# Attention pipelined one chunk deeper, with 64x64 TensorE tiles, whole-array bonus and logits, and two PSUM pairs held for the whole program

## The chip, the cores and the metric

One Trainium2 chip; the program runs on 1 of its cores. The time is the device time of one execution in microseconds (us), lower is better; where several runs are given, their median counts. Engines are named as in the profile: PE is TensorE's matmuls, PEld its weight loads, DVE is VectorE, ACT ScalarE, POOL GpSimd, SP SyncE, which issues most DMAs.

## The reference, cut to what matters

A linear attention with a decaying state feeds a mixture of experts with one expert per token. All is float32.

```python
def _attn_ref(r, k, v, w, u):            # B, H, S, D = 4, 8, 768, 48
    state = zeros((B, H, D, D))
    for t in range(S):
        cur = einsum('bhd,bhe->bhde', u[None] * kt, vt)
        y[:, :, t] = einsum('bhd,bhde->bhe', rt, state + cur)
        state = w[None, :, :, None] * state + einsum('bhd,bhe->bhde', kt, vt)

def _moe_ref(x, w_gate, w_output_gate, w1, w2):   # N, D, E, F = 3072, 384, 8, 1024
    logits = x @ w_gate
    e_idx = argmax(logits, axis=1)
    gate_w = softmax(logits) at e_idx
    eom = 1 / (1 + exp(-(x @ w_output_gate)))
    for e in range(E):
        h = maximum(x[mask] @ w1[e], 0)
        out[mask] = gate_w[mask] * eom[mask, e] * (h @ w2[e])
```

x is y with the heads of a token put side by side. The logits need full float32, since they choose the expert.

## The kernel before, in words

The 3072 tokens are 24 chunks (`NT`) of 128; a sequence of 768 is 6 chunks (`NCH`). A chunk is cut into two halves of 64 tokens (c = 0, 1), and its 8 heads into 4 pairs (q) of two (j = 0, 1). Powers of the decay w are multiplied into r and k beforehand (`prep`, L229, on GpSimd in the loop), so that a half is three plain products:

- `trans` (L254): 8 TensorE transposes of a chunk's scaled r and k, copied from PSUM by ScalarE as RT and KT; `product` (L268): their product rk on VectorE.
- `scores` (L280): KT against RT for each half, 16 calls of 48 rows by 64 columns, into the two-bank PSUM tile `pa`; `causal` (L293) masks them on VectorE into A.
- `state` (L304): k against v for each half, into the other columns of the same `pa`; `carry` (L319) adds the state so far (VectorE) and decays it (GpSimd), once for each half, as T.
- `inter` (L335): RT against T, 16 calls, into the two-bank tile `y`; `intra` (L348): A against v, added to it.
- `coefs` (L359): rk against a small matrix of u, the bonus coefficient of each head; ScalarE copies it with the logits in `strips` (L1328), and `bonus` (L368) is eight ScalarE activations that scale v by it, into vc.
- `output` (L378): VectorE adds y and vc to x, which SP writes to the scratch tensor x_d; then SP loads k, r and v of a chunk five ahead (`load`, `AHEAD`).

State, intra, coefs and logits address the PE array in strips of 32 output columns (`Q32`): state and intra as 64x32 tiles, two calls for what 64 columns hold, coefs and logits as four 128x32 strips. Each float32 matmul call appears in the trace as two weight loads and two matmuls, a transpose as one of each.

The router follows one chunk behind: three transposes of x (`logits_t`, L421), the logits (`logits_into`, L430), and programs of small steps (`Router.group`) for groups of 4 to 6 chunks; `micro` hands their VectorE steps out by a budget, seven times per turn of the loop, and `tensor_slot` their TensorE steps, twice. From turn 18 on two pieces of the first expert's weights are split per turn (`weights0`: ScalarE rounds, GpSimd subtracts the rest). The order of every engine's instructions in this part is the order in which the code is written (`manual_schedule`).

The expert stage: for each of 8 experts x is gathered and transposed, layer 1 runs in eight steps f of nine matmuls (`l1_mm`, L864) and `l1_out` (L877: hh on ScalarE, then hl on VectorE), layer 2 by `l2_rows` or `l2`. Step f writes one half of a two-bank tile: `bank` (L827) takes a new tile for an even f and the other half of it for an odd one, by turns from the two PSUM places that `pa` and `y` had in the attention. Semaphores are generated from the reads and writes of each tile.

Of the kernel before, what the change touches and what calls it, by code (L numbers as in the profile page):

```python
# [8 lines left out]
F32 = mybir.dt.float32  # L9
# [10 lines left out]
C = 128  # L20
NCH = S // C
# [22 lines left out]
Q32 = 32  # L44
# [174 lines left out]
class Attention:  # L219
    def __init__(self, tc, ctx, ps, k, load, x_d):  # L220
# [3 lines left out]
        self.st, self.T, self.vc, self.A, self.rk, self.pa = {}, {}, {}, {}, {}, {}  # L224
# [13 lines left out]
    def first(self):  # L238
# [3 lines left out]
        for n in (1, 0):  # L242
# [3 lines left out]
            RK[n] = self.pw.tile([C, NP, C], F32, name=("RT", "KT")[n])  # L246
# [7 lines left out]
    def trans(self, i):  # L254
# [4 lines left out]
        for n in (0, 1):  # L259
            p = self.ps.tile([C, NP, C], F32, name="ps_t", tag="tr", bufs=2)  # L260
            for q in range(NP):
                nc.tensor.transpose(p[:, q, :], self.st[i][n][:, 2 * q : 2 * q + 2, :], k.ident)
            t = self.pw.tile([C, NP, C], F32, name=("RT", "KT")[n])
            nc.scalar.copy(t, p)  # L264
            out.append(t)
# [9 lines left out]
    def both(self, i):  # L275
        if i not in self.pa:
            self.pa[i] = self.ps.tile([C, 2, 512], F32, name="ps_a", tag="pa", bufs=1)
        return self.pa[i]

    def scores(self, i):  # L280
# [4 lines left out]
        pa = self.both(i)  # L285
# [7 lines left out]
    def causal(self, i):  # L293
        if i >= NT:
# [4 lines left out]
            self.pa[i][:, :, : NP * HB].rearrange("p j (q t) -> p j q t", q=NP),  # L299
# [4 lines left out]
    def state(self, i):  # L304
# [4 lines left out]
        pa = self.both(i)  # L309
        a = NP * HB  # L310
        for q in range(NP):
            for n in range(2):
                for j in range(2):
                    for c in range(1 if i % NCH == NCH - 1 else 2):
                        rows = slice(HB * c, HB * (c + 1))
                        o = pa[HB * j + Q32 * n : HB * j + Q32 * (n + 1), c, a + D * q : a + D * (q + 1)]
                        nc.tensor.matmul(o, Kn[rows, 2 * q + j, Q32 * n : Q32 * (n + 1)], vt[rows, 2 * q + j, :], start=True, stop=True, skip_group_check=True)

    def carry(self, i, c):  # L319
# [4 lines left out]
        U = self.pa[i][:, c, a : a + NP * D].rearrange("p (q e) -> p q e", q=NP)  # L324
# [10 lines left out]
    def inter(self, i):  # L335
        nc = self.tc.nc
        RT = self.st[i][3]
        self.y = self.ps.tile([C, 2, 512], F32, name="ps_y", tag="y", bufs=1)
# [9 lines left out]
    def intra(self, i):  # L348
        nc = self.tc.nc
        vt, A = self.st[i][2], self.A.pop(i)  # L350
        for q in range(NP):
            for j in range(2):
                for n in range(2):
                    for c in range(2):
                        rows = slice(HB * c, HB * (c + 1))
                        o = self.y[HB * c + Q32 * n : HB * c + Q32 * (n + 1), j, D * q : D * (q + 1)]
# [1115 lines left out]
```

## Time and profile before

| | us |
|---|---|
| median of 3 runs | 521.1 |
| lowest and highest run | 520.45 and 526.82 |
| the profiled execution | 525.61 |
| its span, first to last instruction | 523.8 |

| engine | busy us | share of the span | instructions |
|---|---|---|---|
| PE | 402.9 | 77% | 7473 |
| PEld | 367.5 | 70% | 7473 |
| DVE | 224.4 | 43% | 552 |
| ACT | 192.8 | 37% | 505 |
| POOL | 149.7 | 29% | 213 |

The attention loop takes the first 215 us, the expert stage the rest. The two have different limits, so the shares of the whole span say little about either. The profile's times are of the one profiled execution; what lies outside its span is 1.8 us. A line such as L346 is a line of the kernel; a row names the engine, the operation and the tiles, out<-in.

### The profile page before, as it was taken

The numbers are of one execution on the slowest core, as the hardware profiler recorded it, in microseconds if no ns is written. First come the engines' busy times: TensorE is split into PE (matmuls) and PEld (weight loads), VectorE is DVE, ScalarE is ACT, GpSimd is POOL, SyncE is SP. The second block draws the span as 40 slices with busy tenths as digits, with TensorE's granted clock in tenths as the row PEclk, the third lists the DMA queues.
The fourth block names the chain that finished last, engine by engine and source line by source line (L and its number), as shares of the span: only waits on it lengthen the run. The fifth ranks groups of instructions, "written<-read, shape, count | busy, mean of one in ns | idle before, by whom it ended". The sixth has DMA issues, their size and how long they took to land. (4 is left out here: it accounts for less than half of the span.)

```text
span 523.8 us, 17408 instructions
## 1 busy us (share of the span) xinstructions
PE 402.9 (77%) x7473; PEld 367.5 (70%) x7473; DVE 224.4 (43%) x552; ACT 192.8 (37%) x505; POOL 149.7 (29%) x213
## 2 busy tenths in 40 slices
PE   5867776766777687896968888888879788898780
PEld 3756765655666576796967777788869678787680
DVE  4442374375364552364742343433444435334400
ACT  2425353452553634522332432432442424233300
POOL 5533334243342544523130311211212403101010
PEclk9998788988897876799999989989999999898996
DMA  8834445353557423024252342433532623433000
GB/s 144 144 91 102 101 87 110 80 124 81 108 115 194 110 69 104 18 85 151 76 171 61 116 128 93 132 115 99 170 106 81 206 92 115 161 100 121 1 35 18
DMA packets 104991, 55.19 MB, mean 105 GB/s; under 512 B 78911, under 2 KB 102515, under 8 KB 104896
## 3 DMA queue, kind: packets, MB, share of 16 engines
q1 hardware_dynamic: 101472, 44.08, 33.0%
q0 software_dynamic: 3424, 9.82, 5.5%
q8 instruction: 62, 1.02, 0.8%
q14 instruction: 33, 0.27, 0.2%
HBM read 44.45 MB, written 9.76 MB: 103 GB/s over the span
## 5 line engine op out<-in xcount | busy, mean ns | idle before, releaser
L872 PE MATMUL ps_h<-xh,w1h 128*128 128x384 f32 (+4 forms) x216 | 78.6, 364 | 42.6 <-DVE hl L882 41.3
L909 POOL DMA_INDIRECT out_dram<-yo,si x28 | 31.3, 1117 | 180.1 <-ACT yo L906 110.8
L872 PEld LDWEIGHTS ps_h<-xh,w1h 128*128 128x128 f32 x216 | 43.5, 201 | 52.3 <-DVE hl L882 50.5
L873 PE MATMUL ps_h<-xl,w1h 128*128 128x384 f32 (+4 forms) x216 | 75.0, 347 | 0.0
L874 PE MATMUL ps_h<-xh,w1l 128*128 128x384 f32 (+4 forms) x216 | 74.6, 345 | 0.0
L881 ACT ACTIVATE hh<-ps_h 128x384 fp32r<-128x384 f32 (+4 forms) x72 | 34.2, 475 | 105.8 <-PE ps_h L874 97.5
L882 DVE SCALAR_TENSOR_TENSOR hl<-ps_h,hh 128x384 fp32r<-128x384 f32 (+4 forms) x72 | 38.6, 536 | 80.1 <-ACT hh L881 73.7
L815 DVE TENSOR_TENSOR w1l<-raw,w1h 128x768 fp32r<-128x768 f32 x28 | 26.1, 956 | 63.3 <-ACT w1h L814 63.3
L332 POOL TENSOR_TENSOR T<-T,sq 128x192 f32<-128x192 f32 x40 | 20.7, 517 | 111.9 <-DVE T L331 98.7
L272 DVE TENSOR_TENSOR rk<-ps_t,RT 128x512 f32<-128x512 f32 x23 | 15.9, 692 | 67.4 <-ACT KT L264 67.4
L843 POOL DMA_INDIRECT xg<-x_d,gi x28 | 30.0, 1072 | 51.5 <-PE ps_xt L855 36.5
L874 PEld LDWEIGHTS ps_h<-xh,w1l 128*128 128x128 f32 x216 | 43.9, 203 | 0.1
L934 PE MATMUL ps_o<-w2h,hh 128*128 128x384 f32 x128 | 43.6, 341 | 0.0
L873 PEld LDWEIGHTS ps_h<-xl,w1h 128*128 128x128 f32 x216 | 43.4, 201 | 0.1
L936 PE MATMUL ps_o<-w2h,hl 128*128 128x384 f32 x128 | 42.8, 335 | 0.0
L935 PE MATMUL ps_o<-w2l,hh 128*128 128x384 f32 x128 | 42.8, 334 | 0.0
L375 ACT ACTIVATE vc<-v_t,lg 128x48 f32<-128x48 f32 x136 | 32.5, 321 | 0.6
L291 PE MATMUL ps_a<-RT,KT 48*64 48x64 f32 x768 | 20.4, 254 | 13.2 <-ACT KT L264 13.1
L1335 ACT COPY lg<-ps_lg 128x24 f32<-128x24 f32 x18 | 3.2, 178 | 72.3 <-PE ps_lg L434 72.3
L291 PEld LDWEIGHTS ps_a<-RT,KT 48*64 48x64 f32 x768 | 17.1, 163 | 15.9 <-ACT KT L264 15.2
L815 DVE TENSOR_TENSOR w2l<-raw,w2h 128x768 fp32r<-128x768 f32 x28 | 26.8, 956 | 3.2 <-ACT w2h L814 1.9
L357 PE MATMUL ps_y<-v_t,A 64*32 64x48 f32 x1344 | 23.3, 224 | 5.1 <-issue 5.1
(234 smaller groups left out, 823.4 us busy)
## 6 DMA issues: line engine op xcount, KB each, us to landing
raw<-in_moe_w_dram SPq DMA_DIRECT2D x64, 384.0 KB, 3.5
x_d<-x SPq DMA_DIRECT2D x24, 192.0 KB, 2.1
v_t<-in_v_dram SPq DMA_DIRECT2D x21, 192.0 KB, 4.7
k_t<-in_k_dram SPq DMA_DIRECT2D x20, 192.0 KB
r_t<-in_r_dram SPq DMA_DIRECT2D x20, 192.0 KB, 3.4
raw<-in_v_dram SPq DMA_DIRECT2D x3, 192.0 KB
raw<-in_k_dram SPq DMA_DIRECT2D x3, 192.0 KB, 4.4
xg<-x_d,gi POOLq DMA_INDIRECT x28
```

Source lines behind the costliest of these rows:

```text
L291: nc.tensor.matmul(pa[half, j, HB * q : HB * (q + 1)], KT[rows, q, half], RT[rows, q, half], start=True, stop=True, skip_group_check=True)
L375: nc.scalar.activation(vc[:, h, :], vt[:, h, :], AF.Copy, scale=cs[:, h : h + 1])
L815: (eng or nc.vector).tensor_sub(lo, self.raw[i][:, cs], hi)
L872: nc.tensor.matmul(o, wh[:, j, fs], xh, start=(j == 0), stop=False)
L873: nc.tensor.matmul(o, wh[:, j, fs], xl, start=False, stop=False)
L874: nc.tensor.matmul(o, wl[:, j, fs], xh, start=False, stop=(j == KC - 1))
L881: nc.scalar.activation(hh, o, AF.Relu)
L882: nc.vector.scalar_tensor_tensor(hl, o, 0.0, hh, op0=ALU.max, op1=ALU.subtract)
L909: nc.gpsimd.indirect_dma_start(out=self.out, out_offset=bass.IndirectOffsetOnAxis(ap=self.rt.si[:n, q, s : s + 1] if s else self.rt.si0[:n ...
L934: nc.tensor.matmul(o, hh, wh, start=(f == 0), stop=False)
L935: nc.tensor.matmul(o, hh, wl, start=False, stop=False)
L936: nc.tensor.matmul(o, hl, wh, start=False, stop=(f == FC - 1))
```

## The change

In the loop, turn i now transposes chunk i+2 instead of i+1 and forms its state; scores, causal and inter of i+1 stand at the end of the turn, intra and output of i after the coefs and logits instead of before them. Ahead of the loop chunk 1's state, transposes, product and carries and chunk 0's inter are done. `state` and `intra` use 64x64 tiles, `coefs` and `logits_into` the whole array, one call where there were four. `pa` and `y` are allocated once (`k.two`) for the attention and for the layers of the experts; `bank(f)` hands out their four halves in turn. RT has three buffers instead of two, x two instead of three. The rest of the diff passes `self.pa` and `k.two` in place of the tiles taken per chunk.

```diff
         self.tc, self.k, self.ps = tc, k, ps
         self.load, self.x_d = load, x_d
         self.pw = ctx.enter_context(tc.tile_pool(name="att_w", bufs=2))
-        self.st, self.T, self.vc, self.A, self.rk, self.pa = {}, {}, {}, {}, {}, {}
+        self.st, self.T, self.vc, self.A, self.rk = {}, {}, {}, {}, {}
+        self.pa, self.y = k.two
         self.Rn, self.Kn = ([self.pw.tile([C, H, HB], F32, name=f"{nm}{i}", bufs=1) for i in range(n)] for nm, n in (("Rn", 3), ("Kn", 3)))
         for t in self.Kn + self.Rn:
             tc.nc.gpsimd.memset(t[:, :, D:], 0.0)
...
         self.tc.nc.vector.tensor_mul(rk, self.st[i][5], self.st[i][3])
         self.rk[i] = rk
-    def both(self, i):
-        if i not in self.pa:
-            self.pa[i] = self.ps.tile([C, 2, 512], F32, name="ps_a", tag="pa", bufs=1)
-        return self.pa[i]
-
     def scores(self, i):
         if i >= NT:
             return
         nc = self.tc.nc
         RT, KT = self.st[i][3:5]
-        pa = self.both(i)
+        pa = self.pa
         for q in range(NP):
             for j in range(2):
                 rows = slice(HB * j, HB * j + D)
...
             return
         nc = self.tc.nc
         Kn, vt = self.st[i][1:3]
-        pa = self.both(i)
+        pa = self.pa
         a = NP * HB
         for q in range(NP):
-            for n in range(2):
-                for j in range(2):
-                    for c in range(1 if i % NCH == NCH - 1 else 2):
-                        rows = slice(HB * c, HB * (c + 1))
-                        o = pa[HB * j + Q32 * n : HB * j + Q32 * (n + 1), c, a + D * q : a + D * (q + 1)]
-                        nc.tensor.matmul(o, Kn[rows, 2 * q + j, Q32 * n : Q32 * (n + 1)], vt[rows, 2 * q + j, :], start=True, stop=True, skip_group_check=True)
+            for j in range(2):
+                for c in range(1 if i % NCH == NCH - 1 else 2):
+                    rows = slice(HB * c, HB * (c + 1))
+                    o = pa[HB * j : HB * (j + 1), c, a + D * q : a + D * (q + 1)]
+                    nc.tensor.matmul(o, Kn[rows, 2 * q + j, :], vt[rows, 2 * q + j, :], start=True, stop=True, skip_group_check=True)
     def carry(self, i, c):
         if i >= NT or (c == 1 and i % NCH == NCH - 1):
             return
         nc, k = self.tc.nc, self.k
         a = NP * HB
-        U = self.pa[i][:, c, a : a + NP * D].rearrange("p (q e) -> p q e", q=NP)
+        U = self.pa[:, c, a : a + NP * D].rearrange("p (q e) -> p q e", q=NP)
         decay = k.w64.unsqueeze(2).to_broadcast((C, NP, D))
         T = self.pw.tile([C, NP, D], F32, name="T", bufs=5)
         if i % NCH == 0 and c == 0:
...
         self.T[i, c] = T
     def inter(self, i):
+        if i >= NT:
+            return
         nc = self.tc.nc
         RT = self.st[i][3]
-        self.y = self.ps.tile([C, 2, 512], F32, name="ps_y", tag="y", bufs=1)
         T = [None if i % NCH == 0 else self.T[i - 1, 1], self.T[i, 0]]
         for q in range(NP):
             for j in range(2):
...
         vt, A = self.st[i][2], self.A.pop(i)
         for q in range(NP):
             for j in range(2):
-                for n in range(2):
-                    for c in range(2):
-                        rows = slice(HB * c, HB * (c + 1))
-                        o = self.y[HB * c + Q32 * n : HB * c + Q32 * (n + 1), j, D * q : D * (q + 1)]
-                        nc.tensor.matmul(o, A[rows, j, q, Q32 * n : Q32 * (n + 1)], vt[rows, 2 * q + j, :], start=(i % NCH == 0 and c == 0 and q == 0), stop=(q == NP - 1), skip_group_check=True)
+                for c in range(2):
+                    rows = slice(HB * c, HB * (c + 1))
+                    o = self.y[rows, j, D * q : D * (q + 1)]
+                    nc.tensor.matmul(o, A[rows, j, q, :], vt[rows, 2 * q + j, :], start=(i % NCH == 0 and c == 0 and q == 0), stop=(q == NP - 1), skip_group_check=True)
     def coefs(self, i, lg):
         if i >= NT:
             return
         rk = self.rk.pop(i)
         for q in range(NP):
-            for n in range(C // Q32):
-                strip = slice(Q32 * n, Q32 * (n + 1))
-                self.tc.nc.tensor.matmul(lg[strip, 2 * E + 2 * q : 2 * E + 2 * (q + 1)], rk[:, q, strip], self.k.uw[:, q, :], start=True, stop=True, skip_group_check=True)
+            self.tc.nc.tensor.matmul(lg[:, 2 * E + 2 * q : 2 * E + 2 * (q + 1)], rk[:, q, :], self.k.uw[:, q, :], start=True, stop=True, skip_group_check=True)
     def bonus(self, i, cs):
         if i >= NT:
...
     def logits_into(self, pl, xT):
         for j in range(KC):
-            for n in range(C // Q32):
-                strip = slice(Q32 * n, Q32 * (n + 1))
-                self.tc.nc.tensor.matmul(pl[strip, : 2 * E], xT[:, j, strip], self.wg32[:, j, :], start=(j == 0), stop=(j == KC - 1), skip_group_check=True)
+            self.tc.nc.tensor.matmul(pl[:, : 2 * E], xT[:, j, :], self.wg32[:, j, :], start=(j == 0), stop=(j == KC - 1), skip_group_check=True)
     def logits_mm(self, ps, xT, tag):
         pl = ps.tile([C, 512], F32, name="ps_l", tag=tag, bufs=1)
...
         self.ps = ps
         self.op = ctx.enter_context(self.tc.tile_pool(name="m_o", bufs=2))
-    def bank(self, ps, f, name):
-        n, half = f // 2 % 2, f % 2
-        if half == 0:
-            self.two[n] = ps.tile([C, 2, 512], F32, name=f"{name}{n}", tag=("pa", "y")[n], bufs=1)
-        return self.two[n][:, half, :]
+    def bank(self, f):
+        return self.k.two[f // 2 % 2][:, f % 2, :]
     def rows(self, s, q):
         return min(QP, self.caps[s] - q * QP)
...
     ex = Experts(tc, ctx, k, None, w1, w2, x_d, out)
     pctx = ctx.enter_context(ExitStack())
     ps = pctx.enter_context(tc.tile_pool(name="ps", bufs=1, space=PSUM))
+    k.two = [ps.tile([C, 2, 512], F32, name=n) for n in ('ps_a', 'ps_y')]
     with ExitStack() as actx:
         spare = [t[:, a : a + DM] for t in ex.raw for a in (0, DM)] + [ex.xg[0]]
         G = GROUPS[-1][1]
...
         att.prep(2, 0, nc.gpsimd)
         att.prep(2, 1, nc.vector)
         cs0 = [rw.tile([C, 3 * E], F32, name=f"cs{n}") for n in range(2)]
+        att.state(1)
+        att.inter(0)
+        att.trans(1)
+        att.product(1)
+        att.carry(1, 0)
+        att.carry(1, 1)
         strips(-1, None, cs0[0])
         x = None
         for i in range(NT):
             tail = i == NT - 1
-            att.trans(i + 1)
             xT = None
             if x is not None:
                 xT = rt.logits_t(ps, rw, x, "lg", 1)
             micro(i)
-            att.product(i + 1)
+            att.trans(i + 2)
+            att.prep(i + 3, 0, nc.gpsimd)
+            att.prep(i + 3, 1, nc.gpsimd)
             if tail:
                 ex.early_x(ps)
+            att.product(i + 2)
             tensor_slot(1)
-            att.inter(i)
-            att.scores(i + 1)
             micro(i)
             micro(i)
-            att.causal(i + 1)
-            att.prep(i + 3, 1, nc.gpsimd)
-            att.prep(i + 3, 0, nc.gpsimd)
-            att.intra(i)
-            micro(i)
-            x = att.output(i)
-            load(i + AHEAD)
-            load_raw(RAWS)
-            tensor_slot(1)
-            att.state(i + 1)
-            att.carry(i + 1, 0)
-            micro(i)
-            micro(i)
-            att.carry(i + 1, 1)
             if xT is None:
                 strips(i, None, cs0[1])
             else:
...
                 strips(i, xT, dst)
                 if prog:
                     pend.append([prog, V])
+            tensor_slot(1)
+            micro(i)
+            att.intra(i)
+            x = att.output(i)
+            load(i + AHEAD)
+            load_raw(RAWS)
+            att.state(i + 2)
+            att.scores(i + 1)
+            att.carry(i + 2, 0)
+            att.causal(i + 1)
+            att.carry(i + 2, 1)
+            att.inter(i + 1)
+            micro(i)
+            micro(i)
             micro(i)
             if tail:
                 ex.early_mm(ps, 0)
```

## Rows read from the trace of the kernel before

**Rows 1.** Busy time of each engine by stretch, us from the span's start: the attention loop, its first 17 chunks, its last six, the expert stage. The columns are the length, then for each engine the busy us and the number of instructions, the granted TensorE clock as a share of full speed, the DMA engines' mean busy share and GB/s.

```profile
20.00:215.00 195.00, 140.59 (x5848) 123.12 (x5840) 92.95 (x276) 86.03 (x301) 74.02 (x95) 0.84 0.44 103
21.78:160.47 138.69, 98.08 (x4297) 85.38 (x4289) 67.38 (x190) 59.96 (x213) 50.66 (x66) 0.89 0.47 106
160.47:214.80 54.33, 40.53 (x1448) 35.81 (x1448) 24.57 (x84) 25.87 (x88) 23.36 (x29) 0.71 0.36 99
215.00:523.80 308.80, 248.62 (x1413) 234.12 (x1412) 122.04 (x238) 100.74 (x188) 64.92 (x60) 0.95 0.33 104
```

**Rows 2.** The writes of x to the scratch tensor: all 24, with shortest, median and longest duration in ns and the starts of the first and the last; then the eighteenth in the order of time (start, us).

```profile
L387 SPq DMA_DIRECT2D x_d<-x x24: 356/357/362, 21.8 to 214.8; - x24
...
160.47 0.36 SPq L387 DMA_DIRECT2D x_d<-x  x1
```

**Rows 3.** TensorE's waits in the attention loop (20 to 215 us), longest first in total: who waited, for whom; us in total, times, longest. "issue" is time in which the engine waited for nothing that the profile shows.

```profile
PE ps_lg L434 <- issue: 18.9, 12, 2.1
PE ps_a L291 <- ACT KT L264: 12.9, 13, 1.2
PE ps_t L262 <- issue: 7.2, 5, 2.3
PE ps_lg L366 <- issue: 6.7, 4, 2.4
PE ps_y L357 <- issue: 5.1, 5, 1.8
```

**Rows 4.** The same columns as rows 1 for five stretches of the loop, each of which ends where TensorE resumes after an "issue" stall. Then, of the whole page, the engines' busy times and instruction counts, and the DMA queue that brings TensorE's instructions (packets, MB, share).

```profile
78.27:81.44 3.17, 2.18 (x143) 1.96 (x136) 1.82 (x8) 0.00 (x0) 0.74 (x2) 0.66 0.26 75
85.98:90.11 4.13, 2.06 (x146) 1.71 (x135) 2.23 (x9) 0.00 (x0) 1.47 (x3) 1.00 0.22 62
119.07:122.67 3.60, 2.33 (x149) 1.86 (x137) 2.95 (x9) 1.89 (x9) 1.48 (x3) 1.00 0.22 71
122.67:127.21 4.54, 2.72 (x127) 2.35 (x127) 1.38 (x2) 1.55 (x4) 1.55 (x2) 1.00 0.65 128
127.21:131.04 3.83, 2.45 (x128) 2.04 (x128) 1.86 (x8) 0.00 (x0) 1.21 (x3) 0.63 0.19 60
...
PE 402.9 (77%) x7473; PEld 367.5 (70%) x7473; DVE 224.4 (43%) x552; ACT 192.8 (37%) x505; POOL 149.7 (29%) x213
...
q8 instruction: 62, 1.02, 0.8%
```

**Rows 5.** The instructions of one chunk in order of time, some rows of it: start us, us from the first one's start to the last one's end, engine, line, operation, tiles, shape, number; in brackets the idle time before and what ended it.

```profile
81.64 0.66 PE L262 MATMUL ps_t<-ident,Rn 128*128 128x128 f32 x4
...
81.98 1.91 ACT L375 ACTIVATE vc<-v_t,lg 128x48 f32<-128x48 f32 x8
...
82.57 0.49 PE L425 MATMUL ps_x<-ident,x 128*128 128x128 f32 x3
...
82.99 0.68 PE L346 MATMUL ps_y<-T,RT 48*64 48x48 f32 x32
...
84.74 0.47 ACT L427 COPY xT<-ps_x 128x384 f32<-128x384 f32 x1
...
84.89 0.69 PE L291 MATMUL ps_a<-RT,KT 48*64 48x64 f32 x32 [1.22 <-ACT KT L264]
...
85.52 0.92 PE L357 MATMUL ps_y<-v_t,A 64*32 64x48 f32 x64
...
86.37 0.52 PE L590 MATMUL ps_tab<-rhs,ohp 128*128 128x160 bf16 x5
86.48 0.56 DVE L382 TENSOR_TENSOR x<-ps_y,vc 128x384 f32<-128x384 f32 x1
...
86.82 0.81 PE L317 MATMUL ps_a<-v_t,Kn 64*32 64x48 f32 x64
...
87.55 0.43 PE L366 MATMUL ps_lg<-uw,rk 128*32 128x2 f32 x32
...
90.11 0.36 PE L434 MATMUL ps_lg<-wg,xT 128*32 128x16 f32 x19 [2.06 <-issue]
```

**Rows 6.** The one place of the loop where a 128-column float32 weight load is followed by a matmul of few columns, in order of time; and the same two loads by line (shortest, median, longest ns).

```profile
144.39 0.30 PEld L677 LDWEIGHTS ps_ord<-csum,ones 128*128 128x128 f32 x2
...
L677 PEld LDWEIGHTS ps_ord<-csum,ones x2: 186/188/189, 144.4 to 144.5; 128*128 128x128 f32 x2
```

**Rows 7.** The next chunk's first steps in order of time, columns as in rows 5.

```profile
90.41 0.92 PE L262 MATMUL ps_t<-ident,Rn 128*128 128x128 f32 x4
...
91.97 0.85 PE L425 MATMUL ps_x<-ident,x 128*128 128x128 f32 x3
...
92.74 1.11 PE L346 MATMUL ps_y<-T,RT 48*64 48x48 f32 x32
...
93.64 0.87 PE L291 MATMUL ps_a<-RT,KT 48*64 48x64 f32 x32
```

**Rows 8.** The loads of k, r and v by line: from issue to landing.

```profile
DMA to landing us min/median/max: 3.0/4.3/5.5
```

**Rows 9.** TensorE's longest wait in the expert stage (columns as in rows 3), and one such wait in order of time.

```profile
PE ps_h L872 <- DVE hl L882: 41.3, 31, 2.2
...
450.45 0.56 DVE L882 SCALAR_TENSOR_TENSOR hl<-ps_h,hh 128x384 fp32r<-128x384 f32 x1 [1.85 <-ACT hh L881]
...
451.06 0.44 PE L872 MATMUL ps_h<-xh,w1h 128*128 128x384 f32 x1 [1.23 <-DVE hl L882]
```

More of the change, by code (lines that the diff above doesn't have):

```diff
@@ L43 @@
 MID = HB // 2
-Q32 = 32
 ORDER_AT = 14
@@ L245, in first @@
                 nc.tensor.transpose(p[:, q, :], k.raw0["rk"[n]][:, 2 * q : 2 * q + 2, :], k.ident)
-            RK[n] = self.pw.tile([C, NP, C], F32, name=("RT", "KT")[n])
+            RK[n] = self.pw.tile([C, NP, C], F32, name=("RT", "KT")[n], bufs=(3, 2)[n])
             nc.vector.tensor_mul(
@@ L262, in trans @@
                 nc.tensor.transpose(p[:, q, :], self.st[i][n][:, 2 * q : 2 * q + 2, :], k.ident)
-            t = self.pw.tile([C, NP, C], F32, name=("RT", "KT")[n])
+            t = self.pw.tile([C, NP, C], F32, name=("RT", "KT")[n], bufs=(3, 2)[n])
             nc.scalar.copy(t, p)
@@ L298, in causal @@
             a,
-            self.pa[i][:, :, : NP * HB].rearrange("p j (q t) -> p j q t", q=NP),
+            self.pa[:, :, : NP * HB].rearrange("p j (q t) -> p j q t", q=NP),
             self.k.diag.unsqueeze(1).unsqueeze(1).to_broadcast((C, 2, NP, HB)),
@@ L380, in output @@
         self.st.pop(i)
-        x = self.pw.tile([C, DM], F32, name="x", bufs=3)
+        x = self.pw.tile([C, DM], F32, name="x")
         nc.vector.tensor_add(
@@ L794, in __init__ @@
         self.xg = [p.tile([QP, DM], F32, name=f"xg{q}") for q in range(NQ)]
-        self.ys, self.ph, self.two = {}, {}, {}
+        self.ys, self.ph = {}, {}
         self.caps = CAPS[NL]
@@ L865, in l1_mm @@
         nc = self.tc.nc
-        p = self.bank(ps, f, "ps_h")
+        p = self.bank(f)
         o = p[:, : z - a]
@@ L886, in l2 @@
         cap = self.caps[s]
-        p = self.bank(self.ps, j, "ps_z")
+        p = self.bank(j)
         o = p[:, :cap]
```

## The prediction

> **What bounds the kernel now.** I read the busy time by stage first [rows 1], then the times at which chunks leave [rows 2], then TensorE's waits [rows 3], then one chunk in order of time [rows 5]. The attention loop is the stretch to 215 us; what follows is the expert stage, 309 us. The first row of the output goes out at 21.8, the eighteenth at 160.5, the last at about 214.8 [rows 2]: 138.7 / 17 = 8.16 us a chunk, then 54.3 / 6 = 9.06. Per chunk the first 17 have 98.1 / 17 = 5.77 us of busy TensorE; over the whole loop VectorE has 93.0 / 23.9 = 3.9 us a chunk, ScalarE 3.6, GpSimd 3.1 and the DMA engines a share of 0.44 [rows 1]. So TensorE is the long one, and it is still idle for 2.4 us of 8.16.
>
> That idle time has two names [rows 3]. "issue" (18.9 + 7.2 + 6.7 + 5.1 = 37.9 us over the loop, 1.6 us a chunk) is TensorE waiting for nothing that the program asks for. Its place is fixed by counting back from the stalls: five stretches that each end with one hold 127 to 149 matmul records and 127 to 137 weight loads, about 256 instructions, and take 3.2 to 4.5 us, mean 3.85 [rows 4]. The instruction queue brings 1.02 MB in 62 packets, one per 241 of TensorE's 14,946 instructions [rows 4]. I read it as code loading: a block of 256 instructions can't be run faster than the next one arrives. The chunk has 16 calls each for scores and inter, 32 each for state and intra, 16 coefs and 12 logits, each call two weight loads and two matmuls, and 11 transposes of one pair: 4 x 124 + 22 = 518 instructions, 2.02 blocks. 2.02 x 3.85 = 7.8 us of the 8.16. The second name is the wait of scores for ScalarE's copy of KT, 12.9 us, 0.55 a chunk [rows 3]; one stands at 84.89 [rows 5], behind the eight bonus activations.
>
> **The change, part by part.** *Instructions.* State and intra go to 16 calls, coefs to 4, logits to 3: 4 x 71 + 22 = 306, and some 12 for the router, so 318 instead of 530, 1.24 blocks. 1.24 x 3.85 = 4.8 us: code loading no longer sets the chunk, unless one block holds all the dense work. The dense set (intra, state, scores, inter) is 256 instructions in about 2.5 us; about one block in five falls so that it stalls, by up to 3.85 - 2.5 = 1.35 us, half of that on average: 0.2 x 1.24 x 0.65 = 0.15 us a chunk. Bounds: 0, and 1.24 stalls of today's 0.79 (1.6 / 2.02) = 1.0.
>
> *TensorE's work at full clock.* From the chunk at 81.6 [rows 5], start to start: transposes 0.93, x transposes 0.42, intra 0.85, state 0.73, coefs about 0.28 (32 records; 0.43 less what the last one takes beyond its start), logits about 0.35 (19 of 24 records take 0.30 to the next transposes [rows 5, 7]). Scores take 0.63, of which the 32 records need 0.46 (inter: 0.68 less one matmul's 0.22) and 0.17 passes before the next, differently shaped tile starts. With a router step of 0.25 that is 4.9 us. After: state, scores and inter 0.46 each, since 64x64 tiles are what inter has today. Intra I take at 0.92: its call (c, c) always reads and writes the same half, so only two of the four tiles take turns, and each is held for 0.46 / 8 = 0.058 us per record; the lower bound is 0.46. Coefs become 8 records and logits 6, each with a 128-column float32 weight load. The trace has that form once, two loads of 0.188 in 0.30 together, one every 0.11 us [rows 6]: 0.88 + 0.66 = 1.54 us, where strips take 0.63; bounds 0.63, and 14 x 0.195 = 2.7 from the transposes at half clock [rows 7]. Two changes of tile shape a chunk instead of four: 0.34. Sum 0.93 + 0.42 + 0.92 + 3 x 0.46 + 1.54 + 0.34 + 0.25 = 5.8 us. So the work itself grows by 0.9; what shrinks is the waiting. The Trainium skill, "TensorEngine Tiling (Array Packing)", section Theoretical Speedup, speaks against this part: narrow column tiles gain up to 4x side by side, so whole-array coefs and logits could cost 4 x 0.63 = 2.5 us, which would add about 1.0 to the chunk and 23 to the total; the row of 0.11 us decides for 1.54.
>
> *Order.* The transposes of i+2 and the coefs of i+1 now have a whole turn before they are used, so scores no longer wait for KT: 0.55 a chunk gone. What is late next? The y bank: inter(i+1) waits until output(i) has read it, 0.56 us on VectorE [rows 5] and about 0.2 of signalling after intra, while TensorE does state and scores, 0.92: hidden, with 0.15 to spare, and lost by as much as VectorE's router work before output runs over (0 to 0.4; inside the clock term's bounds). State(i+2), scores(i+1) and then both carries and causal on one held tile: VectorE's three steps come after scores, and the next state on TensorE is 3.5 us away. ScalarE's ring: xT 0.47, coefs and logits 1.54, copy 0.18, bonus 1.91 [rows 5], about 0.4 of signalling: 4.5 us, under 5.8. GpSimd now has both preps, 2 us, ahead of the carries' multiplications; the loads they need are issued behind output(i-2)'s write on SP, some 8 us before, and land in 3.0 to 5.5 [rows 8] plus about 2.5 of issuing. Hidden, and what waits on GpSimd is carry(i+2, 1), not TensorE. DMA: 0.44 x 8.2 = 3.6 us of all engines per chunk [rows 1], so 0.6 busy at 6.2. Only around chunk 15, where four 384 KB weight loads come on top, do I charge 1.5 us once.
>
> *Clock.* In the first 17 chunks 5.77 busy against 4.9 at full clock: 0.87 lost, at a granted mean of 0.89 there and 0.84 over the loop, between 1.2 and 2.4 GHz [rows 1]; the clock is half in the chunk at 90.4, after the 2.06 us stall [rows 5, 7]. With stalls that long gone from most chunks I charge 0.25; bounds 0, and 5.8 / 0.89 - 5.8 = 0.7 where nothing improves.
>
> *Held banks in the expert stage.* TensorE waits 41.3 us there for hl, 31 times [rows 9]. The wait is that of the second half of a two-bank tile for the reading of its first half: hl of the half just finished ends at 451.01 and the next half's matmul starts at 451.06, though its own bank was read four steps ago. The changed bank() hands out the same halves of the same two-bank tiles, so by these rows the wait stays. I take 0.
>
> **Sum.** 5.8 + 0.15 + 0.25 = 6.2 us a chunk. 17 x (8.16 - 6.2) = 33.3; the last six, where ScalarE and GpSimd also split weights, keep their 0.9 extra: 6 x (9.06 - 7.1) = 11.8. Before the first output come state(1), the transposes of chunk 2 and the coefs of chunk 1: -1.5, and -1.5 for the loads. Net 42 us: the profiled execution 525.6 to 483.5; the median of the runs, 521.1, by the same 42 to **479 us**. A measurement of this kernel tells about 2% from no change, and this is 8%.
>
> **Rivals.** *By bank in earnest*: dependencies are kept per bank once the tiles are held, and the 41.3 us go as well, 479 - 39 = 440. The Trainium skill, "PSUM — Partial Sum Buffer", section PSUM bank collisions raise a hardware error, has engines collide only in one bank, so nothing in the chip asks for this wait; the trace shows that it is made between banks of one tile all the same. Against: same slices, same tile. 0.12. *The clock falls as far as over the whole loop today*, 0.84: 5.8 / 0.84 + 0.15 = 7.05 a chunk; 17 x 1.1 + 6 x 1.1 - 3 = 22 less, 499. For it: coefs and logits stream 2 and 16 columns behind each weight load. 0.17. *Half clock most of the time*, the slower end: at half clock the sum is 1.56 + 0.77 + 2.7 + 1.8 + 2.7 + 0.34 + 0.4 = 10.3 [rows 7], so from 0.52 of the time at half clock the chunk is longer than 8.16; today it is 2 x (1 - 0.84) = 0.32, and 0.58 in the last six chunks [rows 1]. At 0.70 all through: 5.8 + 0.7 x 4.5 + 0.15 = 9.1, +16 over 17 chunks, 0 over the last six, +3: 540. Against: what went before the falls was a long stall, and these go. 0.05. *No gain*: the y wait and VectorE's carries take the place of the stalls, VectorE's 3.9 plus its waits filling 8 us: 517. 0.04.
>
> **How the numbers follow.** Forecast 0.62. Within it the bounds give 5.3 a chunk (intra at 0.46, clock and code 0) to 7.1 (clock 0.7, code 0.6, short of its bound of 1.0, which would need a stall in every block): 458 to 500. The range goes on to 447 and 503; below it lies most of the bank rival, above it no gain, slower, and a little of the clock rival. Faster 0.90, same 0.05, slower 0.05.
>
> **What would show it.** Chunks leave every 6.2 us; TensorE's "issue" falls from 37.9 to under 10 us; the wait for KT is gone; a coefs record every 0.11 us; intra at 0.9; granted clock over 0.9 in the loop; the wait for hl at 41 as before. Wrong if the clock stays under 0.85, if intra and the whole-array loads cost more than these rows, or if the expert stage is shorter than 305 us.

## The result, and the profile after

The changed kernel takes 478.3 us (median of four runs, 477.6 to 489.5); the ratio to the kernel before is 0.915, interval 0.907 to 0.922. The forecast was 479, range 447 to 503. The profiled execution of the changed kernel is the longest of its runs, 489.5 us: its granted clock over the whole span was 0.921 where the other three had 0.933 to 0.948, so TensorE was at half clock (1.2 instead of 2.4 GHz) for longer in it; e12 below runs the same loop and shows it in a more usual execution.

Stretches of the changed kernel, columns as in rows 1: the first 17 chunks, the last six, the expert stage, one chunk at full clock, one at half clock; then the writes of x (columns as in rows 2) and the queue that brings TensorE's instructions.

```profile
26.60:139.30 112.70, 109.82 (x2589) 106.91 (x2583) 64.78 (x194) 62.96 (x213) 49.24 (x65) 0.85 0.59 131
139.30:182.40 43.10, 37.22 (x797) 35.21 (x792) 26.09 (x79) 24.81 (x81) 24.08 (x30) 0.84 0.42 116
182.40:487.70 305.30, 247.14 (x1392) 233.01 (x1391) 120.83 (x238) 99.20 (x185) 63.80 (x59) 0.95 0.33 105
33.81:39.09 5.28, 5.28 (x158) 5.20 (x153) 2.33 (x5) 3.60 (x12) 2.92 (x4) 1.00 0.70 152
92.71:102.48 9.77, 9.77 (x155) 9.64 (x153) 4.05 (x11) 4.07 (x13) 3.45 (x5) 0.50 0.43 97
...
L379 SPq DMA_DIRECT2D x_d<-x x24: 356/357/1050, 26.6 to 182.4; - x24
...
q8 instruction: 43, 0.70, 0.6%
```

Against [rows 1] and [rows 2], where the same stretches are 138.7, 54.3 and, from 214.8 on, 309.0 us: the first output goes out 4.8 us later, the first 17 chunks lose 26.0 us (6.63 a chunk instead of 8.16), the last six 11.2 (7.18 instead of 9.06), the expert stage 3.7. 4.8 - 26.0 - 11.2 - 3.7 = -36.1 us, which is the difference of the two spans. TensorE, idle for 2.4 us of each chunk before, is now busy for 109.8 of 112.7 us: a chunk without a router step is 5.28 us long with TensorE busy for all of it.

TensorE's waits in the loop of the changed kernel (columns as in rows 3), then those for hl in its expert stage:

```profile
PE ps_y L341 <- DVE x L374: 2.4, 3, 1.7
PE ps_tab L580 <- DVE rhs L575: 2.2, 1, 2.2
...
PE ps_y L341 <- issue: 1.0, 1, 1.0
...
PE ps_x L417 <- issue: 0.3, 1, 0.3
...
PE ps_a L859 <- DVE hl L869: 23.7, 16, 2.2
PE ps_y L859 <- DVE hl L869: 18.4, 16, 1.3
```

The 37.9 us of "issue" and the 12.9 of KT in [rows 3] have become 1.3 and nothing. What is left is the router's data and the y bank, each a few times. The wait for hl is where it was, 42.1 us against 41.3 in [rows 9].

One chunk of the changed kernel at full clock, in order of time (columns as in rows 5), to be set against [rows 5]:

```profile
108.72 0.55 PE L417 MATMUL ps_x<-ident,x 128*128 128x128 f32 x3
109.10 0.60 PE L262 MATMUL ps_t<-ident,Rn 128*128 128x128 f32 x4
...
109.97 0.95 PE L358 MATMUL ps_lg<-uw,rk 128*128 128x2 f32 x8
110.79 0.82 PE L424 MATMUL ps_lg<-wg,xT 128*128 128x16 f32 x6
111.54 1.07 PE L351 MATMUL ps_y<-v_t,A 64*64 64x48 f32 x29
...
112.49 0.59 PE L311 MATMUL ps_a<-v_t,Kn 64*64 64x48 f32 x28
...
112.97 0.59 PE L286 MATMUL ps_a<-RT,KT 48*64 48x64 f32 x28
...
113.44 0.63 PE L341 MATMUL ps_y<-T,RT 48*64 48x48 f32 x27
```

Start to start: x transposes 0.38, transposes 0.87, coefs 0.82, logits 0.75, intra 0.95, state 0.48, scores 0.47, and 0.56 for inter to make up the 5.28.

### The profile page after: what moved, and what is told of

Its sections match the earlier page's. It is cut to its first block, busy times and chain, and to the rows that moved or that the text cites. A ratio compares the mean times of both kernels' runs of the same rounds, so it can differ in the third digit from the quotient of the medians.

```text
span 487.7 us, 12378 instructions
## 1 busy us (share of the span) xinstructions
PE 414.1 (85%) x4993; PEld 392.1 (80%) x4993; DVE 222.8 (46%) x552; ACT 196.3 (40%) x505; POOL 148.8 (31%) x213
## 5 line engine op out<-in xcount | busy, mean ns | idle before, releaser
L859 PE MATMUL ps_a<-xh,w1h 128*128 128x384 f32 (+4 forms) x108 | 39.7, 367 | 23.7 <-DVE hl L869 23.7
L859 PE MATMUL ps_y<-xh,w1h 128*128 128x384 f32 (+4 forms) x108 | 38.8, 359 | 18.4 <-DVE hl L869 18.4
L859 PEld LDWEIGHTS ps_a<-xh,w1h 128*128 128x128 f32 x108 | 21.7, 201 | 28.6 <-DVE hl L869 28.4
L923 PE MATMUL ps_o<-w2h,hl 128*128 128x384 f32 x128 | 42.8, 335 | 0.0
L922 PE MATMUL ps_o<-w2l,hh 128*128 128x384 f32 x128 | 42.8, 334 | 0.0
L859 PEld LDWEIGHTS ps_y<-xh,w1h 128*128 128x128 f32 x108 | 21.5, 199 | 23.2 <-DVE hl L869 23.1
L869 DVE SCALAR_TENSOR_TENSOR hl<-ps_y,hh 128x384 fp32r<-128x384 f32 (+4 forms) x36 | 19.3, 537 | 41.5 <-ACT hh L868 41.4
L861 PE MATMUL ps_a<-xh,w1l 128*128 128x384 f32 (+4 forms) x108 | 37.8, 350 | 0.0
L860 PE MATMUL ps_a<-xl,w1h 128*128 128x384 f32 (+4 forms) x108 | 37.3, 346 | 0.0
L860 PE MATMUL ps_y<-xl,w1h 128*128 128x384 f32 (+4 forms) x108 | 36.5, 338 | 0.0
L861 PE MATMUL ps_y<-xh,w1l 128*128 128x384 f32 (+4 forms) x108 | 36.4, 337 | 0.0
L351 PE MATMUL ps_y<-v_t,A 64*64 64x48 f32 x672 | 28.6, 244 | 0.0
```

The source lines that it names most:

```text
L859: nc.tensor.matmul(o, wh[:, j, fs], xh, start=(j == 0), stop=False)
L860: nc.tensor.matmul(o, wh[:, j, fs], xl, start=False, stop=False)
L861: nc.tensor.matmul(o, wl[:, j, fs], xh, start=False, stop=(j == KC - 1))
L869: nc.vector.scalar_tensor_tensor(hl, o, 0.0, hh, op0=ALU.max, op1=ALU.subtract)
L922: nc.tensor.matmul(o, hh, wl, start=False, stop=False)
L923: nc.tensor.matmul(o, hl, wh, start=False, stop=(f == FC - 1))
```

## The experiments

**e1: the two pairs by turns in the experts.** Is the wait for hl a wait for the other half of the same pair, as the prediction read it?

```diff
-        return self.k.two[f // 2 % 2][:, f % 2, :]
+        return self.k.two[f % 2][:, f // 2 % 2, :]
```

> The changed kernel with one line changed: the steps of layer 1 take the two held PSUM pairs by turns (step f uses pair f mod 2), so that the step before never wrote the other half of the same pair. Theory (the wait for hl is a wait of the program for the whole two-bank tile, as the prediction has it): TensorE's 42.1 us of waiting for hl in the expert stage go, since hl of f-2 is done a whole step of about 3 us earlier; the expert stage falls from 305 to about 265 us, the total to 438 us (430 to 445). The attention loop is unchanged. Rival (the banks of layer 1 were already used by bank and TensorE waits there for VectorE's other work, the weight splits, or for the weights): the wait only changes its name, total 470 to 480.

Measured: about 436 us (432.3 to 443.2; a fourth execution, of 2054 us, is left out), beside 524.4 of the kernel before on that chip. The expert stage of its profiled execution is 258.1 us long instead of 305.3, and 3.6 us of waiting for hl are left. So the wait was the program's, and nearly all of its 42 us lay in one line. e12 is the same kernel on another chip; its rows are shown there.

**e2: fewer instructions in the old order.** The kernel before with state, coefs and logits in the new forms (state's loop over n goes, as in the change):

```diff
         for q in range(NP):
-            for n in range(C // Q32):
-                strip = slice(Q32 * n, Q32 * (n + 1))
-                self.tc.nc.tensor.matmul(lg[strip, ...], rk[:, q, strip], ...)
+            self.tc.nc.tensor.matmul(lg[:, ...], rk[:, q, :], ...)
...
```

> The kernel before with its old order, PSUM tiles and buffers, but with state in 64x64 tiles and coefs and logits on the whole array; intra stays in 64x32 tiles. 4 x 87 + 22 + 12 = 382 TensorE instructions a chunk, 1.49 blocks of 256. Theory (instructions first, order second): 1.49 x 3.85 = 5.7 us of code loading no longer sets the chunk; TensorE's issue stalls fall from 37.9 to under 10 us, the wait for the copy of KT stays at 0.55 a chunk or grows, a chunk takes about 7.2 us, total about 500 us (490 to 507). Rival (the new order is what gains): the KT wait takes over what the stalls leave, total 512 to 521.

Measured: 521.4 us, ratio 0.988 (0.982 to 0.995): the upper end of the rival's range. Its waits in the loop, one chunk's KT wait, and two stretches of the loop, at nearly full and at half clock:

```profile
PE ps_a L291 <- ACT KT L264: 23.0, 17, 2.1
...
PE ps_lg L429 <- issue: 0.6, 1, 0.6
PE ps_lg L363 <- issue: 0.5, 1, 0.5
...
78.03 0.69 PE L291 MATMUL ps_a<-RT,KT 48*64 48x64 f32 x32 [1.31 <-ACT KT L264]
...
30.70:125.70 95.00, 78.58 (x2363) 71.26 (x2363) 49.49 (x136) 45.76 (x162) 38.61 (x50) 0.96 0.51 111
132.90:153.30 20.40, 20.40 (x388) 19.02 (x382) 8.80 (x37) 7.34 (x26) 6.13 (x8) 0.51 0.48 118
```

The stalls went as expected (37.9 to 1.1 us). At nearly full clock the chunk is what was worked out (13 chunks in 95.0 us, 7.3), but the wait for KT grew from 12.9 to 23.0 us, and at half clock a chunk takes 10.2 us (two in 20.40). I read the miss so: before, the code loading held a chunk at about 8 us whatever the clock was, and with that gone half clock counts in full. The trace of the kernel before bears it out, in two stretches, each from one stall to the next (columns as in rows 1):

```profile
64.17:72.90 8.73, 5.33 (x255) 4.62 (x254) 6.40 (x29) 3.76 (x14) 2.74 (x5) 1.00 0.44 96
72.90:81.44 8.54, 7.50 (x255) 6.64 (x256) 5.82 (x14) 3.74 (x13) 3.69 (x5) 0.60 0.43 95
```

Both hold two blocks of instructions; at a granted clock of 0.60 TensorE is busy for 2.2 us more, and yet the stretch does not get longer.

**e3: the new order with the old instructions.** State, intra, coefs and logits of the changed kernel back in strips of 32 columns.

```diff
+Q32 = 32
...
-            for j in range(2):
-                for c in range(2):
-                    rows = slice(HB * c, HB * (c + 1))
-                    o = self.y[rows, j, D * q : D * (q + 1)]
+            for j in range(2):
+                for n in range(2):
+                    for c in range(2):
+                        rows = slice(HB * c, HB * (c + 1))
+                        o = self.y[HB * c + Q32 * n : HB * c + Q32 * (n + 1), j, D * q : D * (q + 1)]
```

> The changed kernel with its new order and held tiles, but with state and intra in 64x32 tiles and coefs and logits in 128x32 strips as before: 530 instructions a chunk, 2.07 blocks of 256. Theory (code loading, 3.85 us a block): 8.0 us a chunk, issue stalls back to 35 us or more, total 505 to 515 us. Rival (TensorE's own work sets the chunk; strips cost 0.63 us a chunk for coefs and logits where the whole array takes 1.67, state 0.73 instead of 0.46): about 0.8 us a chunk shorter than the changed kernel, 455 to 465 us.

Measured: 517.7 us, ratio 0.987 (0.983 to 0.992), a little above the theory's range and far from the rival's. Its issue waits in the loop:

```profile
PE ps_a L313 <- issue: 30.7, 16, 3.1
PE ps_lg L431 <- issue: 3.1, 5, 1.0
...
PE ps_lg L363 <- issue: 3.0, 4, 1.4
PE ps_x L422 <- issue: 2.7, 1, 2.7
PE ps_y L343 <- issue: 1.9, 1, 1.9
PE ps_y L354 <- issue: 1.7, 3, 1.0
```

Together 43.1 us, more than the 37.9 of [rows 3]. So fewer instructions in the old order (e2, which keeps intra in 64x32 tiles) are worth 1.2%, the new order with the old instructions 1.3%, and the two together 8.5%: before, the chunk had two limits of nearly the same length, code loading (7.8 us) and the order's chain with its KT wait (7.3 us at full clock), and taking one away uncovers the other.

**e4: strips for coefs and logits only.** More instructions, but less work for TensorE.

```diff
-            self.tc.nc.tensor.matmul(pl[:, : 2 * E], xT[:, j, :], ...)
+            for n in range(C // Q32):
+                strip = slice(Q32 * n, Q32 * (n + 1))
+                self.tc.nc.tensor.matmul(pl[strip, : 2 * E], xT[:, j, strip], ...)
...
```

> The changed kernel with only coefs and logits back in 128x32 strips: 402 instructions a chunk, 1.57 blocks, while TensorE's work falls from 5.28 us at full clock to 5.28 - 1.67 + 0.63 = 4.24. Theory (the longer of code loading and work): 1.57 x 3.85 = 6.0 us a chunk, with issue stalls of 1 us or more a chunk, so within 2% of the changed kernel: 470 to 488 us, although TensorE works 1 us less per chunk. Rival (TensorE's work alone): 4.24 plus today's clock loss, 23 x 1.0 less: 455 us.

Measured: 483.4 us, ratio 0.923 (0.915 to 0.932), as the theory has it. Its longest issue waits in the loop, and its first 17 chunks:

```profile
PE ps_a L287 <- issue: 8.0, 10, 2.3
PE ps_y L352 <- issue: 5.3, 6, 2.1
...
24.40:129.90 105.50, 87.15 (x3272) 80.04 (x3266) 64.66 (x193) 62.98 (x214) 49.23 (x65) 0.94 0.63 138
```

TensorE is busy for 87.2 us of 17 chunks, where e12, with the whole array and nearly the same clock (0.95), has 98.9; and the chunk is 105.5 / 17 = 6.2 us long against e12's 6.0, 1.57 blocks of 3.85 us being 6.0. The work saved came back as waiting. The stalls are a little smaller than expected: with two rows not shown (2.9 and 1.3 us) they come to 17.5 us over the loop, some 0.75 a chunk.

**e8: instructions that do next to nothing.** The direct test of code loading, on e1's kernel.

```diff
                     nc.tensor.matmul(o, A[rows, j, q, :], vt[rows, 2 * q + j, :], ...)
+                    for n in range(4):
+                        nc.tensor.matmul(self.pa[HB * (1 - c) : HB * (2 - c), c, 500 + n : 501 + n], self.k.warm[rows, :HB], self.k.warm[rows, :1], ...)
```

> The kernel of e1 with 64 bf16 matmuls of one column more per chunk, into unused columns, placed in intra on the two of the four 64x64 tiles that intra leaves idle: 128 TensorE instructions more a chunk, 446 or 1.74 blocks of 256, and little work (128 instructions at the spacing that state shows, 64 in 0.41 us, are at most 0.8 us, of which intra's own idle time covers a part). Theory (code loading, 3.85 us a block): a chunk can't be shorter than 6.7 us even at full clock, where e1 shows 5.28; issue stalls of about 1 us a chunk appear, total 455 to 465 us. Rival (the number of instructions doesn't matter, only their work): chunks of 5.3 to 6.0 us at full clock, no issue stalls, total 436 to 452 us.

Measured: 472.5 us, ratio 0.903 (0.894 to 0.913); e12, without the idle instructions, 0.821. Two chunks of it one after the other at full clock, the stall in the second, the two stretches from that stall to the next and from there to the one after, TensorE's issue waits in the loop, and the whole loop:

```profile
91.00:96.40 5.40, 5.40 (x219) 5.32 (x213) 2.56 (x5) 3.60 (x13) 2.93 (x4) 1.00 0.69 153
96.40:103.60 7.20, 5.67 (x219) 5.40 (x213) 2.59 (x6) 3.65 (x13) 2.41 (x3) 1.00 0.50 112
...
98.64 0.32 PE L341 MATMUL ps_y<-T,RT 48*64 48x48 f32 x6 [1.53 <-issue]
98.64:120.98 22.34, 20.24 (x640) 19.40 (x641) 14.47 (x47) 11.50 (x39) 8.27 (x13) 0.85 0.51 112
120.98:136.40 15.42, 15.23 (x384) 14.82 (x384) 4.78 (x14) 7.05 (x24) 4.85 (x7) 0.67 0.41 88
...
PE ps_y L341 <- issue: 5.3, 5, 1.8
PE ps_a L286 <- issue: 2.9, 3, 2.1
...
26.10:218.00 191.90, 179.89 (x4853) 173.81 (x4848) 88.78 (x272) 89.28 (x293) 73.24 (x95) 0.70 0.44 104
```

64 more matmuls and 64 more weight loads cost a chunk 0.12 us where nothing stalls (5.40 against 5.28), and the next chunk, with the same work, takes 7.20 because of a 1.53 us stall. The place of the stalls is fixed by the count: between 98.64 and 120.98 there are 640 matmuls and as many loads, 5 x 256 instructions, then 384 of each, 3 x 256, and all eight stalls of the loop stand 2, 3 or 5 blocks of 256 apart. That the number of instructions alone brings the stalls is shown. The size is not as expected: the time lies above both ranges, there are only eight stalls, 8.2 us in all, and a chunk at full clock took 5.40 us where 6.7 was to be the least; only the two chunks together, 6.3 each, come near it. At half clock a chunk's own work is longer than that (9.77 us in the changed kernel), and a granted clock of 0.70 is half clock for 60% of the loop, which leaves less time in which loading can be the limit. Of the (0.903 - 0.821) x 519 = 43 us that the kernel takes more than e12 most go with that clock. How the added instructions bring the clock down was not separated from the stalls.

**e5: tiles taken anew in the experts.**

```diff
-    def bank(self, f):
-        return self.k.two[f // 2 % 2][:, f % 2, :]
+    def bank(self, ps, f):
+        n, half = f // 2 % 2, f % 2
+        if half == 0:
+            self.two[n] = ps.tile([C, 2, 512], F32, name=("ps_a", "ps_y")[n], tag=("pa", "y")[n], bufs=1)
+        return self.two[n][:, half, :]
```

> The changed kernel, but in the expert stage bank() takes a new two-bank tile for every even step, as in the kernel before; the attention keeps the two held pairs. Theory (holding the tiles changes no wait, since both forms hand out the same halves in the same order): the wait for hl stays at 41 to 43 us, total 478 us (473 to 485, the same as the changed kernel). Rival (the held tiles save something on their own): 5 us or more slower than the changed kernel.

Measured: 476.3 us, ratio 0.916 (0.911 to 0.922), the changed kernel's 0.915 again, with 23.8 + 18.4 = 42.2 us of waiting for hl. Holding the pairs does nothing for the expert stage; the attention, which holds them in e5 too, was not run without it.

**e7: coefs and logits in two strips of 64**, on e1's kernel: as in e4 with `range(2)` and `HB` for `C // Q32` and `Q32`.

> The kernel of e1 with coefs and logits in two strips of 64 columns (14 calls instead of 7): 346 instructions a chunk, 1.35 blocks, 5.2 us of code loading. Theory (a whole-array float32 load holds the array 0.11 us, two halves can be loaded side by side): coefs and logits take about 1.0 us a chunk at full clock instead of 1.67, the work falls to 4.6 us, but code loading then sets 5.2, so the total stays at 430 to 438 us. Rival (the halves are loaded one after the other, each as long as the whole): coefs and logits take 3.3 us, a chunk 6.9 us at full clock, total 465 us or more.

Measured: 425.2 us (417.3 to 425.9; before: 519.4). Two chunks of it, and, in the second, coefs and the step behind the logits:

```profile
36.90:46.40 9.50, 9.50 (x326) 9.00 (x323) 4.75 (x9) 7.11 (x25) 5.35 (x7) 1.00 0.75 161
...
43.75 0.63 PE L360 MATMUL ps_lg<-uw,rk 128*64 128x2 f32 x16
...
44.68 1.07 PE L351 MATMUL ps_y<-v_t,A 64*64 64x48 f32 x29
```

The two steps take 0.93 us from start to start instead of 1.57, and a chunk 4.75, faster than either theory had it: 4.75 is below the 5.2 us that code loading was to set, without a stall in these two chunks. But 5.2 counts 12 router instructions, and these chunks have no router step: 2 x 334 instructions in 9.50 us are 3.64 us a block, within the 3.2 to 4.5 of single blocks [rows 4]. Whether 5.2 holds as a mean is not settled; with router steps and half clock the first 17 chunks take 6.1 us each here and 5.9 in e9. Whole array, two strips and four strips (in e4, from 75.99 to 76.57; the prediction's estimate was 0.63) take 1.57, 0.93 and 0.58 us. The Trainium skill, "TensorEngine Tiling (Array Packing)", section Theoretical Speedup, gives up to 2x and up to 4x for tiles this narrow; these rows give 1.7 and 2.7.

**e6, e10, e11: the clock.** In e1 the router's small steps wait a little for VectorE (0.44 us at 57.65, 0.28 at 87.35), and the clock falls soon after, at 59.4 and 90.1. e6 hands them out later and moves one turn of VectorE's work behind the output; e10 and e11 do one of the two each.

```diff
-            tensor_slot(1)
+            tensor_slot(2)
...
-            tensor_slot(1)
-            micro(i)
+            tensor_slot(2)
             att.intra(i)
             x = att.output(i)
+            micro(i)
```

> The kernel of e1 (436 us) with the router's TensorE steps handed out only when two of the seven VectorE turns have passed since they became due (before: one), and with the VectorE turn that stood ahead of the output put behind it. Theory (the falls of the clock follow the short waits ahead of the router's small matmuls: in e1 the clock is half from 59.4, 90.1, 120.8 and 144.7 us, each 2 to 4 us behind such a wait at 57.7, 87.4, 117.1, 141.8): without these waits TensorE stays at full clock longer, granted clock of the loop from 0.87 to over 0.93, total 420 to 428 us. Rival (the clock falls anyway): only the waits themselves go, about 4 us, clock of the loop 0.85 to 0.89, total 430 to 438 us.

> e1 with the first of e6's two edits alone: the router's TensorE steps one VectorE turn later. Theory (it is the wait for the router's data ahead of its small matmuls that goes before the falls of the clock): granted clock of the loop over 0.92 as in e6 (0.94), total 422 to 427 us. Rival (it is the wait of inter for the output, which the other edit shortens): clock as in e1 (0.87), 432 to 440 us.

> e1 with the second of e6's two edits alone: the VectorE turn behind the output instead of ahead of it. Theory: the falls stay where the router waits, clock of the loop 0.86 to 0.89, total 432 to 439 us. Rival (this edit is what keeps the clock): over 0.92, 422 to 427 us.

**e12: e1 again**, on a third chip, where the kernel before takes 519.8 us as on theirs (519.4 and 520.4):

> The kernel of e1 once more, because e1 was timed on another chip (before: 524 us there, 519 to 520 us where e6, e7 and e9 to e11 ran) and what the two edits of e6 gain over it hangs on that. If e6's edits keep the clock up, e1 takes 432 to 438 us here too, 0.83 to 0.84 of before, and the clock is half for 35 us or more of the loop in its profile. If the difference was one of chips or of executions, 422 to 428 us, 0.81 to 0.825 of before.

Measured: e6 422.9 us, ratio 0.814 (0.809 to 0.819); e10 425.7, 0.819 (0.812 to 0.827); e11 426.4, 0.817 (0.812 to 0.822); e12 431.4, 0.821 (0.814 to 0.828). The loop of e6 in two parts, a stretch of it and its longest wait, then the loop of e12 in the same two parts and its expert stage:

```profile
27.00:125.60 98.60, 95.41 (x2589) 93.01 (x2583) 65.82 (x192) 62.90 (x213) 50.28 (x65) 0.98 0.65 143
125.60:167.50 41.90, 36.05 (x789) 33.70 (x790) 26.38 (x83) 25.34 (x82) 24.92 (x30) 0.86 0.50 135
...
63.21:145.13 81.92, 75.16 (x1989) 72.70 (x1986) 63.73 (x190) 54.28 (x184) 46.57 (x60) 1.00 0.67 153
...
PE ps_y L341 <- DVE x L374: 3.5, 4, 1.2
```

```profile
26.00:128.00 102.00, 98.86 (x2589) 95.83 (x2583) 64.98 (x195) 63.03 (x213) 49.13 (x65) 0.95 0.64 143
128.00:171.00 43.00, 39.71 (x789) 37.71 (x790) 25.96 (x79) 25.52 (x82) 24.92 (x30) 0.75 0.44 121
171.00:424.80 253.80, 233.54 (x1394) 227.33 (x1392) 120.19 (x238) 98.78 (x183) 63.82 (x59) 0.98 0.40 126
```

e6's time and clock (0.94 over its loop) are what its theory named, and TensorE stays at full clock for 82 us on end. But e12 takes most of the difference away: there e1's kernel has 0.821 of before, all four intervals overlap, and either edit alone gives the same. That e6's clock was up is a row; that the router's waits bring the falls is not shown. It can't be short waits as such: within those 82 us inter waited three times for the output, 1.0 to 1.2 us each, and the clock stayed. Nor is it the router's wait by itself: e12 has e1's wait of 0.28 us, at 86.62, and its clock was at full from 63.9 to 114.9. e11, which leaves the router's steps where they were, has a clock of 0.91 in its loop, between its theory and its rival; e10's profiled execution, 452.5 us, can't answer, since the granted clock was 0.85 in it where it was not at half. What brings the falls is left open.

**e9: e6 and e7 together.**

> e6 and e7 together: the pairs by turns, the router's steps later, coefs and logits in strips of 64. In e6 the chunk at full clock is 5.28 us, all of it TensorE's work; in e7 the work is 4.73, and chunks without a router step take 4.73 to 5.43. Theory (code loading of 346 instructions, 1.35 x 3.85 = 5.2 us a chunk, is the limit once the work is below it): 0 to 0.25 us a chunk less than e6, 417 to 423 us, with some issue stalls. Rival (nothing else limits): 4.73 instead of 5.28, 23 x 0.55 = 13 us less than e6, 410 us.

Measured: 417.9 us, ratio 0.797 (0.789 to 0.805), the fastest of all, at the theory's time and with 1.5 + 1.0 + 0.7 = 3.2 us of issue stalls. That does not show code loading to be its limit: its loop, 139.8 us, had a granted clock of 0.88 where e6's, 140.5 us, had 0.94, so the clock may have taken what the rival forecast. It beats the changed kernel by 0.915 - 0.797 = 0.118 of before, some 61 us, of which 0.915 - 0.821, some 49 us, are e1's line.

## Why the prediction was right, step by step

- **Code loading as the bound: right.** Issue fell from 37.9 to 1.3 us, the instruction packets from 62 to 43; e3 and e4 bring the stalls back with the calls, e8 by added instructions alone. The 0.15 us a chunk charged for what is left of it was 0.06. The rows give stalls 256 instructions apart and 1.02 MB / 62 = 16.5 KB a packet [rows 4]; the Trainium skill, "Runtime: NRT & Kernel Launch", section Instruction fetch mechanics, has the same block and says that crossing one is mostly hidden. Here it is not: it cost 1.6 us a chunk, and the measurement decides.
- **Order: right, and needed.** The KT wait went altogether; e2 shows that without the new order it would have taken most of the gain, which the prediction, pricing it at 0.55 a chunk, did not see.
- **TensorE's work: 0.3 too high.** Forecast 5.8 with a router step of 0.25, measured 5.28 without one, so 5.55 against 5.28. Coefs and logits were 1.57 (1.54 forecast from one row of two loads), intra 0.95 (0.92), state and scores 0.48 and 0.47 (0.46). The term that was mis-sized is the two changes of tile shape: 0.34 forecast, and all that is left for them is the 0.56 of inter less its 0.46, 0.1.
- **Clock: charged about right for e12's first 17 chunks, too little for the profiled execution.** A chunk is 5.28 us at full and 9.77 at half clock, so half clock loses 46% of its time. At 0.85 granted, half clock holds 2 x 0.15 x 112.7 = 34 us, 15.6 lost, 0.92 a chunk; in e12's loop at 0.95 it is 10.2 us, 4.7 lost, 0.28 a chunk, against 0.25 forecast. The remainder is 6.63 - 0.92 - 5.28 = 0.43 and 6.0 - 0.28 - 5.28 = 0.44: router steps, short waits and loading, where 0.25 + 0.15 stood in the forecast. So 6.2 a chunk was met by 6.0 and 6.6, and the last six by 7.2 for 7.1. The sign named, over 0.9 in the loop, did not come: 0.85 in the profiled execution and 0.89 over e12's loop. The reason given, that the falls of the clock follow long stalls and go with them, did not hold: the stalls went and the clock fell all the same.
- **The start: mis-sized.** 1.5 us were charged for the steps ahead of the first output and it came 4.8 us later: they run at half clock, two sets of transposes and two of coefs among them, coefs at 1.70 us as the first row, of the changed kernel, shows, against 0.95 in the chunk above. 1.70 is what coefs take in this kernel's half-clock chunk too (at 95.12). Its profile gives a granted clock of 1.00 at 19.13, but in e12 the same steps, equally long (coefs 1.70 at 18.51), stand at 0.50, as the second row shows:

```profile
19.13 1.70 PE L358 MATMUL ps_lg<-uw,rk 128*128 128x2 f32 x8
```

```profile
16.00:26.00 10.00, 10.00 (x121) 9.89 (x117) 2.56 (x5) 6.28 (x22) 4.01 (x6) 0.50 0.32 56
```

The kernel before ran its first steps as slowly: four transposes take 0.91 us there from start to start (15.32 to 16.23), where the changed kernel's take 0.85 at half and 0.44 at full clock.

- **The y bank, ScalarE, GpSimd, the loads: hidden, as worked out.** The y wait came three times, 2.4 us. A loss of 1.5 us around chunk 15 can't be told from the clock.
- **Held banks: right.** 42.1 us of waiting stayed, the expert stage fell by 3.7 of 309; e5 shows that holding is worth nothing there and e1 that the wait was between two halves of one pair. The rival "by bank in earnest" named the time that this is worth (440) and gave it to the wrong edit.
- **The total: nearer than its terms.** The median fell by 42.8 us where 42 was forecast, the profiled execution by 36.1. The work was 0.3 a chunk too high, some 6 us, and the 3.7 us of the expert stage stood at nothing; against that stand 3.3 us too little at the start and a clock that takes 0.28 a chunk in one execution and 0.92 in another. That 479 was met within 1 us is in part luck.

What e1's line frees is more than the wait. Groups by line from 215 us on, first of the changed kernel, then of e12: the first matmuls of layer 1's steps on ps_y (columns: busy us, mean ns, idle time before):

```profile
L859 PE MATMUL ps_y<-xh,w1h 128*128 128x384 f32 x48 | 18.1, 378 | 9.4 <-DVE hl L869 9.4
```

```profile
L859 PE MATMUL ps_y<-xh,w1h 128*128 128x384 f32 x48 | 16.2, 338 | 0.0
```

The stage goes from 305.3 us (305.7 in e4) to 253.8, 51.5 less, where the wait was 42.1; TensorE's busy time falls with it from 247.1 to 233.5, at a granted clock of 0.98 instead of 0.95.

## What to carry to other kernels

Count TensorE's instructions per step of the loop beside its busy time: where "issue" waits recur at a fixed count, the calls per step are the bound, and wider tiles that make the engine work longer can still be the faster ones. Two limits of nearly equal length hide each other, so an edit that is worth nothing alone may be half of a large gain, and is to be tried together with its partner. A wait between two halves of one allocation is a wait of the program: handing out the allocations by turns, not their halves, moved it a whole step away in one line.

## What the runs showed of the hardware that was not expected

- A stretch of light instructions is not free: 128 added ones cost 0.12 us a chunk in work, and the whole loop then ran at a granted clock of 0.70 instead of the 0.95 and 0.75 of e12's two parts. They count in full for the stalls, which stand whole blocks of 256 instructions apart in e8.
- Half clock after the stalls had gone: 34 of 113 us in the profiled execution of the changed kernel, with TensorE busy for 97% of the stretch.
- Whole-array float32 loads with 2 and 16 columns behind them take 0.10 and 0.125 us each; in two strips of 64 the same products take 0.6 of that, in four of 32 less than 0.4.
